# A gate for the first MLP's blocks: waiting for converted weights instead of converting in front of them

## The chip, the cores and the metric

The kernel runs on one core of a Trainium2 chip. The metric is the device time of one execution in microseconds (us). Engine names are those of the profile: PE (TensorE, matmuls), PEld (its weight loads), DVE (VectorE), ACT (ScalarE), POOL (GpSimd), SP (SyncE, which issues most DMAs). Each engine works through its own queue in order.

## What is computed

A linear recurrence over 768 steps for 4 x 8 heads of size 40, then two MLPs over 3072 tokens of width 320 with 2048 hidden units. In the reference's words, cut:

```python
for t in range(S):
    y[t] = r[t] @ state
    state = state * w[t] - outer(state @ a[t], b[t]) + outer(v[t], k[t])
x = y as (3072, 320)
x = (max(x @ w_in1, 0) ** 2) @ w_out1
h = x @ w_in2
return (h * clip(h + 3, 0, 6) / 6) @ w_out2
```

The weights come in as float64 and are converted to pairs of float32 on the chip: a high part and a low part.

## The kernel before, in words

**The recurrence** is cut into 12 chunks of 64 steps for each of 4 batches, 48 steps of a loop over `i`. One turn of that loop is called a *slot* here. A slot holds stages in the order of a string, `ORDER`: `rhs`, `ys` (of the slot before), `umm`, `f1`, `kt`, `pre`, `gmm`, `mp`, `st`, `vumm`, `mx`; `f1`, `kt` and `pre` prepare a slot that comes eight later. Between them stand four places `M`. The PE instructions of `rhs` (L670) are the first of a slot. ACT copies their result (RHS, L672) for `umm` (L680); ACT and DVE make GV (L700, L691) for `ys` (L710). Every four slots a triangular inverse is computed on DVE (L627, L630; ML, INV, TMP), in 62 small steps that are dealt out over the places.

**The first MLP** is cut into 6 groups of 512 tokens (each is the output of 8 slots) and 16 blocks of 128 hidden units. For a block there are two pieces: the first product (`project_in`, 8 matmuls into h, then r, g and gs on ACT and DVE), called IN here, and the second (`out1`, 8 matmuls into three accumulators o), called OUT. `piece()` issues one of the two; `fill(i)` calls it at each place `M`. `load` fetches a group's tokens (xr), `prep` splits them (`split_x`: xm, xh on ACT, L207 and L209). Before any group is ready, or while it is held, `fill` issues idle products instead (`keep_warm`, 4 at each place); once a group is ready an empty place stays empty.

**The conversion** (`convert`) is a generator over 32 items: 16 blocks, w_in and w_out of each (part 0 and 1). An item is a raw load (bits, on SP), five to seven elementwise steps on DVE, ACT and POOL (L127 to L156), and a store of the low part (LI or LO, in DRAM). It yields about four times an item, and two steps of it are taken at each place `M`. The first 16 items (blocks 0 to 7) run in slots 0 to 7, with scratch of their own. From block 8 on an item waits until the MLP has come near its block, since its low part goes straight into the tile (wd) that the matmuls will read, and that has two buffers. Later groups load the low parts again from DRAM (wl, L169, on ACT's queue), two blocks ahead.

`ahead` gets the weights of the block two further on, and through `block_in` and `block_out` calls `need`: if that block isn't converted, `need` takes as many steps of the generator as it lacks, on the spot. So around blocks 8 to 15 two to four items are issued in one go, in the middle of a slot.

After the recurrence the pieces follow each other alone, first the rest of the first MLP, then the second MLP (the same with its own weights); the second conversion starts when 94 INs of the first MLP are out.

Of the kernel before, what the change touches and what calls it, by code (L numbers as in the profile page):

```python
# [25 lines left out]
NF = 16  # L26
# [7 lines left out]
class Moe:  # L34


    def __init__(self, tc, ctx, pctx, consts):
        nc = self.nc = tc.nc
        self.pool = ctx.enter_context(tc.tile_pool(name="m_buf", bufs=1))
        self.rot = ctx.enter_context(tc.tile_pool(name="m_rot", bufs=2))  # L40
        self.pso = pctx.enter_context(tc.tile_pool(name="m_pso", bufs=1, space=PSUM))
        self.psh = pctx.enter_context(tc.tile_pool(name="m_psh", bufs=1, space=PSUM))
        self.xpool = ctx.enter_context(tc.tile_pool(name="m_x", bufs=2))
        self.hold = 0
        self.pso4, self.gpool, self.depth = None, self.rot, 2
        self.plan, self.wi, self.wo, self.gs = [], {}, {}, {}
        self.loaded, self.early, self.age = deque(), 0, 0
        self.aside, self.steps = iter(()), 0
        self.pairs = {}
        self.ready = self.n_in = self.n_out = self.s_in = self.s_out = 0  # L50
        self.cst = self.pool.tile([128, 36], FP32, name="cst")
        nc.sync.dma_start(out=self.cst, in_=consts["cst"])
# [233 lines left out]
    def ahead(self, n_in, n_out):  # L286
# [5 lines left out]
        while self.s_out <= min(n_out, len(self.plan) - 1):  # L292
            g, raw, f = self.plan[self.s_out]
            self.wo[self.s_out] = self.block_out(raw, f)
            self.s_out += 1

    def piece(self):

        n, o = self.n_in, self.n_out
        if self.loaded:  # L300
            self.loaded[0]["age"] -= 1
        if self.hold and self.ready:
            self.hold -= 1
        self.try_prep()
        if self.hold and self.ready:
            return False
        first = self.early == 0 and n % NF == 0 and o < n
        if n < self.ready and n - o < self.depth and not first:
            g, _, f = self.plan[n]
            self.gs[n] = self.project_in(self.wi.pop(n), g["x"], g["second"], lambda: self.ahead(n + 2, -1))  # L310
            self.n_in += 1
            self.try_prep()
        elif o < n:
            g, _, f = self.plan[o]
            if f == 0:
                g["acc"] = [self.acc(k, g["second"]) for k in range(4 if g["second"] else 3)]
            (self.out2 if g["second"] else self.out1)(g["acc"], self.wo.pop(o), self.gs.pop(o), f)
            if f == NF - 1:
                g["finish"](g["acc"])
            self.n_out += 1  # L320
            self.ahead(-1, o + 2)
        else:
            return False
        for _ in range(self.steps):
            next(self.aside, None)
        return True
# [126 lines left out]
def rwkv_moe_moe2_kernel(ctx, tc, pre_in, vr_in, v_in, nat, ident_d, mask_d, cst_d, w1_in, w1_out, w2_in, w2_out, out,  # L453
# [4 lines left out]
    NCH, NB = pre_in.shape[0], pre_in.shape[1]  # L458
# [7 lines left out]
    moe = Moe(tc, ctx, mctx, consts)  # L466
# [62 lines left out]
    def load_main(i):  # L529
        c, b = divmod(i, NB)  # L530
        for h, P in enumerate((PA, PB) if i < NS else ()):
            PV = slice(64, 128) if h == 0 else slice(0, 64)
            nc.sync.dma_start(out=VS[i % NB][PV, :, h, :], in_=v_in[c, b, h])
            nc.sync.dma_start(out=VR[i % 3][P, :, :, 64 - 64 * h:128 - 64 * h], in_=vr_in[c, b, h])
# [223 lines left out]
    def tick(n=1):  # L758
        for _ in range(n):
            if not gens or gens[0][1]:  # L760
                return
            if skip[0]:
                skip[0] -= 1
                return
            step = next(gens[0][0], "end")
            if step == "end":
                gens.popleft()
                done[0] += 1
                start_inv()
            elif step:  # L770
                gens[0][1] = step

    def slot_end():
        if gens and gens[0][1] > 0:
            gens[0][1] -= 1
# [14 lines left out]
    def pre_a():  # L790
        if jj[0] < NS:
            f1(jj[0])

    def pre_b():
        if jj[0] < NS:
            kt(jj[0])

    def pre_c():
        j = jj[0]
        if j >= NS:  # L800
            return
        adv(j + 1)
        if j % NB == NB - 1:
            gens.append([inv_gen(j // NB), None])
            start_inv()
        jj[0] += 1
# [7 lines left out]
    def fill(i):  # L814
        if not moe.piece() and (moe.ready == 0 or moe.hold):
            keep_warm(idle if i else 0)

    def store1(g):
        def go(acc):
            for k in range(3):  # L820
                o = moe.rot.tile([128, TOK], FP32, tag="rgr"[k], name="os")
                (nc.vector.tensor_copy if k % 2 else nc.scalar.copy)(out=o, in_=acc[k])  # L822
                nc.sync.dma_start(out=X2[g][128 * k:128 * k + 128], in_=o)
        return go
# [13 lines left out]
    with tc.manual_schedule():  # L838
# [33 lines left out]
        def cstep(n):  # L872
            for _ in range(n):
                next(moe.aside, None)
# [57 lines left out]
        groups1 = [moe.group(raw1, X1[g], 0, store1(g)) for g in range(NG)]  # L932
        STAGES = {"rhs": rhs, "umm": umm, "gmm": gmm, "vumm": vumm, "ys": ys, "st": st, "mp": merge_p, "mx": merge_x}

        def need_inv(i):
            while done[0] <= i // NB:
                if gens[0][1]:
                    slot_end()
                tick()

        for i in range(NS + 1):
            for word in (ORDER if moe.ready else ORDER0).split():
                name, _, off = word.partition(":")
                k = i + int(off or 0)
                if name == "M":
                    fill(i)
                    slot_end()
                    for k in range(5):
                        tick()
                        if k < 2:  # L950
                            cstep(1)
                elif name == "load":
                    if 0 <= k <= NS:
                        load_main(k)
                elif name == "f1":
                    pre_a()
                elif name == "kt":
                    pre_b()
                elif name == "pre":
                    pre_c()  # L960
                elif 0 <= k < NS:
                    if name == "mp":
                        need_inv(k)
                    STAGES[name](k)
                    if name == "ys" and k % (2 * NB) == 2 * NB - 1:
                        moe.load(groups1[k // (2 * NB)])
                        if k < 2 * NB:
                            moe.loaded[0]["age"] = 6
            if i == 2 * NB - 1:
                moe.need(raw1, n_early)  # L970
        actx.close()
        wp2 = ctx.enter_context(tc.tile_pool(name="m_w2", bufs=1))
        hctx = ctx.enter_context(ExitStack())
# [83 lines left out]
def build(arrays):  # L1057
    import concourse.bacc as _bacc
    import concourse.tile as _tile
    from concourse import mybir as _mybir  # L1060

    nc = _bacc.Bacc("TRN2", target_bir_lowering=False, num_devices=1)
    args, ins = [], {}
    for name in _INS:
        a = arrays[name]
        ins[f"in_{name}_dram"] = a
        args.append(nc.dram_tensor(f"in_{name}_dram", a.shape, _mybir.dt.from_np(a.dtype), kind="ExternalInput").ap())
    args.append(nc.dram_tensor("out_0_dram", (3072, 320), _mybir.dt.float32, kind="ExternalOutput").ap())
    with _tile.TileContext(nc) as tc:
        rwkv_moe_moe2_kernel(tc, *args[:3], args[3:9], *args[9:])  # L1070
    return nc, ins
# [8 lines left out]
```

## Time and profile before

| | |
|---|---|
| median of 3 runs | 1436.09 us (1433.65 to 1438.65) |
| the profiled execution | 1440.75 us |
| its span | 1439.0 us |
| PE busy | 1186.5 us, 82% |
| DVE, ACT, POOL busy | 55%, 42%, 28% |
| mean granted clock of PE | 0.895 |

A row of the page gives shares over the whole span; the stages have different bounds. A granted clock of 1.0 is 2.4 GHz, 0.5 is 1.2 GHz. PE's busy time counts pipelined matmuls whose ends are modelled.

### The profile page before, as it was taken

What the parts mean: (1) busy time and instruction counts of PE and PEld (TensorE: products, weight loads), DVE (VectorE), ACT (ScalarE), POOL (GpSimd) and SP (SyncE); (2) the same over time, 40 slices, a digit from 0 to 9 for tenths busy, and PEclk for the clock granted to TensorE, in tenths of its full rate; (3) what the DMA queues carried; (4) which work ended last, traced back from release to release, by engine and by line L of the source; (5) the groups of instructions that cost most, each with busy time, mean ns of one, the idle gap of its engine ahead of it and who ended that gap; (6) DMA issues with size and microseconds to landing.
All of it is one profiled execution on the core that took longest, in us unless ns stands there. A gap on an engine that the chain in (4) does not pass through costs nothing.

```text
span 1439.0 us, 25925 instructions
## 1 busy us (share of the span) xinstructions
PE 1186.5 (82%) x9682; PEld 1003.3 (70%) x9682; DVE 792.5 (55%) x1841; ACT 610.6 (42%) x1456; POOL 409.4 (28%) x612
## 2 busy tenths in 40 slices
PE   3177787976679899999999899797666899999994
PEld 3166776855568677777778778585544798888984
DVE  7823667586575949575765733345554444344432
ACT  4144443535445445445444433344444433344331
POOL 5685454344534333333332000003333000000000
PEclk9668689987689999999999999898778999999997
DMA  5534556636537475665655442634333443434331
GB/s 127 135 79 132 124 123 141 145 94 145 131 95 164 104 143 150 138 122 137 140 133 107 128 111 76 213 110 149 121 112 99 135 130 118 138 104 136 102 118 50
DMA packets 270150, 178.43 MB, mean 124 GB/s; under 512 B 202944, under 2 KB 228160, under 8 KB 270016
## 3 DMA queue, kind: packets, MB, share of 16 engines
q1 hardware_dynamic: 238656, 106.95, 32.5%
q10 hardware_dynamic: 29312, 63.45, 14.7%
q0 software_dynamic: 2048, 6.29, 1.1%
q8 instruction: 79, 1.29, 0.4%
q14 instruction: 55, 0.45, 0.1%
HBM read 140.99 MB, written 35.65 MB: 123 GB/s over the span
## 4 chain that ended last, share of the span: by engine, by line
PE 36%; DVE 13%; DMA 11%; ACT 4%; POOL 3%; issue 3%; SPq 1%; ACTq 0%; DVEq 0%; POOLq 0%
PE h L221 7%; PE h L223 3%; PE o L261 3%; DMA DT<-TB 3%; DMA wl<-LO 3%; PE o L262 3%; DMA wl<-LI 3%; PE o L260 2%; DVE TMP L627 2%; DVE INV L630 2%; PE o L248 2%; POOL cv L139 2%; PE h L225 2%; PE h L224 2%; PE o L250 2%
## 5 line engine op out<-in xcount | busy, mean ns | idle before, releaser
L221 PE MATMUL h<-xm,wi_hi 128*128 128x512 f32 x384 | 165.9, 432 | 38.5 <-ACT wi_hi L70 38.5
L239 DVE TENSOR_TENSOR gs<-g,gs 128x512 fp32r<-128x512 f32 x192 | 143.8, 749 | 80.7 <-ACT gs L233 68.8
L221 PE MATMUL h<-xm,wl 128*128 128x512 f32 x336 | 134.5, 400 | 22.5 <-DMA wl<-LI 22.5
L627 DVE TENSOR_TENSOR TMP<-ML,INV 128x126 f32<-128x126 f32 (+22 forms) x341 | 109.7, 322 | 70.1 <-DMA ML<-DT 50.9
L596 POOL TENSOR_TENSOR RK<-RK,mask 64x256 f32<-64x256 f32 x96 | 74.0, 771 | 255.6 <-ACT RK L595 244.4
L231 DVE SCALAR_TENSOR_TENSOR g<-r,h 128x512 f32<-128x512 f32 x96 | 65.9, 686 | 124.5 <-ACT r L230 124.4
L236 DVE TENSOR_TENSOR g<-r 128x512 f32<-128x512 f32 x96 | 66.6, 694 | 112.1 <-ACT r L235 112.1
L260 PE MATMUL o<-wo_hi,gs 128*128 128x320 f32 x384 | 123.0, 320 | 4.8 <-ACT os L822 3.0
L262 PE MATMUL o<-wo_hi,gs 128*128 128x320 f32 x384 | 122.6, 319 | 1.9 <-DVE gs L239 1.9
L223 PE MATMUL h<-xr,wi_hi 128*128 128x512 f32 x384 | 123.2, 403 | 0.0
L230 ACT ACTIVATE r<-h,cst 128x512 f32<-128x512 f32 x96 | 66.0, 687 | 122.2 <-PE h L225 117.8
L139 POOL TENSOR_TENSOR cv<-bits,cv 128x384 int32<-128x384 int32 (+1 forms) x48 | 44.7, 931 | 254.2 <-DVE bits L127 183.4
L221 PEld LDWEIGHTS h<-xm,wi_hi 128*128 128x128 f32 x384 | 76.9, 200 | 49.9 <-ACT wi_hi L70 40.5
L630 DVE TENSOR_TENSOR INV<-INV,TMP 128x126 f32<-128x126 f32 (+22 forms) x341 | 106.7, 313 | 7.9
L235 ACT ACTIVATE r<-h 128x512 f32<-128x512 f32 x96 | 57.2, 596 | 104.7 <-PE h L225 95.1
L261 PE MATMUL o<-wl,gs 128*128 128x320 f32 x320 | 99.9, 312 | 0.4
L233 ACT CAST gs<-g 128x512 fp32r<-128x512 f32 x96 | 59.5, 620 | 71.7 <-DVE g L231 71.7
L221 PEld LDWEIGHTS h<-xm,wl 128*128 128x128 f32 x336 | 64.1, 191 | 34.9 <-DMA wl<-LI 26.6
L223 PEld LDWEIGHTS h<-xr,wi_hi 128*128 128x128 f32 x384 | 75.1, 196 | 17.6
L248 PE MATMUL o<-gs,wo_hi 128*128 128x512 f32 x192 | 86.9, 452 | 0.0
L557 POOL TENSOR_TENSOR RK<-IN,EE 40x256 f32<-40x256 f32 x82 | 69.8, 852 | 57.6 <-DVE EE L545 54.3
L260 PEld LDWEIGHTS o<-wo_hi,gs 128*128 128x128 f32 x384 | 74.9, 195 | 14.1 <-ACT gs L233 6.6
(174 smaller groups left out, 2763.8 us busy)
## 6 DMA issues: line engine op xcount, KB each, us to landing
wl<-LI ACTq DMA_DIRECT2D x84, 384.0 KB
IN<-in_pre_dram SPq DMA_DIRECT2D x44, 418.0 KB
wl<-LO ACTq DMA_DIRECT2D x44, 384.0 KB
wl<-LO ACTq DMA_DIRECT2D x40, 320.0 KB
bits<-in_moe_w_in_dram SPq DMA_DIRECT2D x32, 384.0 KB
bits<-in_moe_w_out_dram SPq DMA_DIRECT2D x32, 320.0 KB
VR<-in_vr_dram SPq DMA_DIRECT2D x96, 80.0 KB
DT<-TB SPq DMA_DIRECT2D x24, 256.0 KB
```

The costliest lines, as they stand in the source:

```text
L139: nc.gpsimd.tensor_tensor(out=q, in0=t.bitcast(I32), in1=q, op=ALU.add)
L221: nc.tensor.matmul(h, w[p][:, k], xm[:, k], start=(k + p == 0), stop=False)
L223: nc.tensor.matmul(h, hi[:, k], lo[:, k], start=False, stop=False)
L239: nc.vector.tensor_tensor(out=gs[:, 1], in0=g, in1=gs[:, 0].bitcast(FP32), op=ALU.subtract)
L248: nc.tensor.matmul(acc[d], hi, gs[:, 0], start=a, stop=False)
L260: nc.tensor.matmul(acc[q], gs[:, 0, s], hi, start=a, stop=False)
L261: nc.tensor.matmul(acc[q], gs[:, 0, s], lo[:, 0:DM], start=False, stop=False)
L262: nc.tensor.matmul(acc[q], gs[:, 1, s], hi, start=False, stop=z)
L557: e.tensor_tensor(out=rk[P, :, 64 * h:64 * h + 64], in0=a[P], in1=E[P, :, 0:64], op=ALU.mult)
L596: nc.gpsimd.tensor_tensor(out=o, in0=o, in1=mask[P].unsqueeze(1).to_broadcast([64, NP, 64]), op=ALU.mult)
L627: eng.tensor_tensor(out=tmp, in0=ml[:, s, s + 1:32].unsqueeze(2).to_broadcast([128, n, w]), in1=inv[:, s, 0:w].unsqueeze(1).to_broadcast([ ...
L630: eng.tensor_tensor(out=inv[:, s + 1:32, 0:w], in0=inv[:, s + 1:32, 0:w], in1=tmp, op=ALU.subtract)
```

## The change

A function `short(n, o)` says whether the weights of block n (first product) or o (second product) are not yet converted. `piece()` asks it for the two blocks that `ahead` would fetch and, as long as `gate` is set, issues nothing at that place if it says so; the conversion then goes on with its two steps a place. `gate` is cleared at the end of the recurrence. A group's tokens, which were loaded as soon as they were written, now wait in a list until all items are converted and the MLP has begun the group two before it.

```diff
+    def short(self, n, o):
+        for k, extra in ((n, 2), (o, 4)):
+            _, raw, f = self.plan[min(k, len(self.plan) - 1)]
+            if raw is self.raw and self.converted < 2 * (f - f % 2) + extra:
+                return True
+        return False
...
-        if self.hold and self.ready:
+        if self.hold and self.ready or self.gate and self.short(n + 2, o + 2):
             return False
...
                     if name == "ys" and k % (2 * NB) == 2 * NB - 1:
-                        moe.load(groups1[k // (2 * NB)])
-                        if k < 2 * NB:
-                            moe.loaded[0]["age"] = 6
+                        waiting.append(k // (2 * NB))
+
+                if waiting and (moe.converted == 2 * NF and moe.n_in >= (waiting[0] - 1) * NF or waiting[0] == 0):
+                    g = waiting.popleft()
+                    moe.load(groups1[g])
+                    if g == 0:
+                        moe.loaded[0]["age"] = 6
...
+        moe.gate = False
         actx.close()
```

**Place one: ACT between slots 13 and 14.** In the program before, from the end of a piece's conversion to the copy RHS of slot 14 (r and gs belong to an IN, bits, wi_hi and wd to the conversion, GV, TB and RHS to the recurrence):

```order
L138 ACTIVATE bits<-bits 128x384
L700 COPY GV_138<-a 128x8x40
L235 ACTIVATE r<-h 128x512
L237 ACTIVATE gs<-r 128x512
L130 ACTIVATE bits<-bits 128x384
L70 CAST wi_hi<-bits 128x384
L138 ACTIVATE bits<-bits 128x384
L70 CAST wi_hi<-bits 128x384
L663 ACTIVATE TB_129<-a 128x4x32
L672 COPY RHS_137<-a 128x160
```

The same place in the changed program, up to the next copies of the recurrence (its lines are 8 further on):

```order
L235 ACTIVATE r<-h 128x512
L237 ACTIVATE gs<-r 128x512
L708 COPY GV_138<-a 128x8x40
L130 ACTIVATE bits<-bits 128x320
L671 ACTIVATE TB_129<-a 128x4x32
L680 COPY RHS_137<-a 128x160
L138 ACTIVATE bits<-bits 128x320
L690 ACTIVATE VR_136<-a 40x4x64 x2
```

Of the four conversion steps between GV and RHS one is left; the others stand in later slots.

**Place two: ACT where the recurrence ends.** Before: the last copy GV, and the split of group 5 (xm, xh) two INs later.

```order
L700 COPY GV_138<-a 128x8x40
L235 ACTIVATE r<-h 128x512
L237 ACTIVATE gs<-r 128x512
L169 DMA wl<-LI_7_206 128x768
L235 ACTIVATE r<-h 128x512
L237 ACTIVATE gs<-r 128x512
L169 DMA wl<-LO_7_214 128x768
L207 CAST xm<-xr 128x512 x2
L209 CAST xh<-xr 128x512
L235 ACTIVATE r<-h 128x512
L237 ACTIVATE gs<-r 128x512
L169 DMA wl<-LI_0_199 128x768
```

In the changed program the last copy GV is followed by blocks of group 4:

```order
L708 COPY GV_138<-a 128x8x40
L235 ACTIVATE r<-h 128x512
L237 ACTIVATE gs<-r 128x512
L169 DMA wl<-LI_1_200 128x768
L830 COPY os<-o_8140 128x512
L830 COPY os<-o_8142 128x512
L235 ACTIVATE r<-h 128x512
L237 ACTIVATE gs<-r 128x512
L169 DMA wl<-LO_1_208 128x768
```

and the split of group 5 stands in the middle of that group's blocks:

```order
L169 DMA wl<-LI_4_203 128x768
L169 DMA wl<-LO_3_210 128x768
L235 ACTIVATE r<-h 128x512
L237 ACTIVATE gs<-r 128x512
L207 CAST xm<-xr 128x512 x2
L209 CAST xh<-xr 128x512
L235 ACTIVATE r<-h 128x512
L237 ACTIVATE gs<-r 128x512
L169 DMA wl<-LI_5_204 128x768
```

Twelve INs and twelve OUTs more stand behind the recurrence than before; the loads of weights and the split go with them.

## Rows read from the trace of the kernel before

**Rows 1.** The page's 40 slices: PE busy and PE's granted clock, in tenths.
```profile
PE   3177787976679899999999899797666899999994
PEclk9668689987689999999999999898778999999997
```
**Rows 2.** Timeline of PE: start, us, instruction; first of slots 0, 8, 12, 23.
```profile
71.93 0.97 PE L670 MATMUL a<-VS,RK 128*64 128x40 f32 x14
...
216.53 0.66 PE L670 MATMUL a<-VS,RK 128*64 128x40 f32 x16
...
280.36 0.67 PE L670 MATMUL a<-VS,RK 128*64 128x40 f32 x16
...
508.93 0.66 PE L670 MATMUL a<-VS,RK 128*64 128x40 f32 x16
```
**Rows 3.** Stretches between slots: length, busy times, PE's clock, DMA share, GB/s.
```profile
core 0: us, PE busy (x) PEld busy (x) DVE busy (x) ACT busy (x) POOL busy (x), PEclk, DMA share, GB/s
71.90:216.50 144.60, 113.66 (x1182) 102.34 (x1180) 69.06 (x183) 62.34 (x184) 86.54 (x132) 0.73 0.48 114
136.40:216.50 80.10, 61.18 (x625) 55.16 (x624) 49.81 (x138) 32.71 (x97) 42.39 (x60) 0.74 0.51 116
216.50:247.40 30.90, 24.43 (x315) 22.00 (x314) 21.89 (x66) 13.42 (x42) 12.25 (x22) 0.94 0.63 137
280.40:508.90 228.50, 179.55 (x1718) 148.50 (x1716) 156.69 (x400) 109.92 (x293) 96.59 (x132) 0.85 0.54 125
299.50:429.80 130.30, 89.72 (x784) 74.30 (x781) 90.52 (x225) 63.34 (x165) 59.94 (x77) 0.76 0.49 118
429.80:492.00 62.20, 59.17 (x628) 49.05 (x624) 42.29 (x112) 31.92 (x87) 24.01 (x37) 0.97 0.61 142
```
**Rows 4.** PE's waits in 299.5 to 429.8: total us, times, longest.
```profile
PE a L680 <- ACT RHS L672: 28.0, 5, 6.1
PE a L710 <- ACT GV L700: 11.3, 4, 3.1
```
**Rows 5.** Timeline of ACT in slot 13; in brackets idle before and releaser.
```profile
304.54 0.55 ACT L70 CAST wi_hi<-bits 128x384 fp32r<-128x384 f32 x1 [0.72 <-DVE bits L146]
...
308.72 0.54 ACT L70 CAST wi_hi<-bits 128x384 fp32r<-128x384 f32 x1 [3.16 <-DVE bits L146]
...
309.34 0.28 ACT L672 COPY RHS<-a 128x160 f32<-128x160 f32 x1
```
**Rows 6.** Groups of DVE in 280 to 430, by line and shape: busy us, mean ns.
```profile
L239 DVE TENSOR_TENSOR gs<-g,gs 128x512 fp32r<-128x512 f32 x12 | 10.0, 836 | 0.9
L236 DVE TENSOR_TENSOR g<-r 128x512 f32<-128x512 f32 x12 | 8.7, 723 | 3.7 <-ACT r L235 3.7
```
**Rows 7.** DVE's waits in 429.8 to 558.9.
```profile
DVE TMP L627 <- DMA ML<-DT: 17.2, 2, 8.8
```
**Rows 8.** DVE's waits in 136.4 to 216.5.
```profile
DVE bits L127 <- issue: 9.3, 1, 9.3
...
DVE bits L156 <- DMA LO<-bits: 7.0, 1, 7.0
DVE bits L127 <- DMA LI<-bits: 5.8, 1, 5.8
```
**Rows 9.** Timeline of PE after the recurrence: the first matmuls of two INs.
```profile
933.62 0.39 PE L221 MATMUL h<-xm,wi_hi 128*128 128x512 f32 x1
...
937.25 0.39 PE L221 MATMUL h<-xm,wi_hi 128*128 128x512 f32 x1
```
**Rows 10.** PE's waits in 898 to 925.
```profile
PE h L221 <- DMA wl<-LI: 10.2, 1, 10.2
```
**Rows 11.** Timeline of ACT in 903 to 924.
```profile
905.80 1.14 ACT L207 CAST xm<-xr 128x512 fp32r<-128x512 f32 x2 [4.45 <-DMA xr<-X]
908.45 0.62 ACT L209 CAST xh<-xr 128x512 fp32r<-128x512 f32 x1 [1.51 <-DMA xr<-X]
...
909.60 0.34 ACTq L169 DMA_DIRECT2D wl<-LI  x1
```

More of the change, by code (lines that the diff above doesn't have):

```diff
@@ L43, in __init__ @@
         self.xpool = ctx.enter_context(tc.tile_pool(name="m_x", bufs=2))
-        self.hold = 0
+        self.hold, self.gate = 0, True
         self.pso4, self.gpool, self.depth = None, self.rot, 2
@@ L933, in rwkv_moe_moe2_kernel @@
         STAGES = {"rhs": rhs, "umm": umm, "gmm": gmm, "vumm": vumm, "ys": ys, "st": st, "mp": merge_p, "mx": merge_x}
+        waiting = deque()
         def need_inv(i):
```

## The prediction

> **What bounds the kernel now.** I read the page's slices first: PE is busy eight or nine tenths in most slices from the thirteenth on, but six and seven tenths in slices nine to twelve, where its granted clock is lower too [rows 1]. To tell what lies there I took the starts of the first PE instruction of a slot, the rhs products (L670), as marks [rows 2], and asked for the stretches between such marks [rows 3]. A slot is one turn of the loop over `i`; it has four places for a piece of the first MLP, a first product (8 matmuls, called IN below) or a second product (OUT). Four slots without conversion (429.8 to 492.0) take 62.2 us at a clock of 0.97: PE is the bound there. The five slots from 299.5 take 130.3 us at 0.76, with PE busy 89.7. Who ended PE's waits there stands in [rows 4]: ACT, 39.3 us, at the copies RHS (L672) and GV (L700). The reason stands in ACT's own rows [rows 5]: it waits 3.16 us at L70 for the DVE's half of a conversion step, and the RHS copy that PE needs is queued behind that. So in this stretch the conversion of blocks 8 to 15, forced in bulk between two pieces, stands in front of the recurrence, and PE, whose queue is in order, does nothing else meanwhile. After the recurrence PE runs the MLPs back to back: what is taken out of the slots must be done there.
>
> **The change part by part.** The gate is decided while the program is written; it adds no instruction and no semaphore wait. The first difference in the order is in slot 12, and in slots 12 to 22 (280.4 to 508.9) the new program has 10 INs and 10 OUTs where the old one has 22 of each; the 16 items of conversion (eight blocks, two parts) are all in these slots in both. From slot 23 on every slot has its four pieces again, and the missing 12 INs and 12 OUTs stand after the last attention instruction. Each engine has as many instructions as before. So there are three terms.
>
> *First term, slots 12 to 22, now 228.5 us [rows 3].* Not shown by the trace is a slot with scattered conversion, about one pair of pieces and no idle products, so I bound it. From below: DVE is busy 156.7 us here; the 12 INs that leave take a g (0.723) and a gs (0.836) each [rows 6], 18.7 us, and 138.0 stay. Three inverses begin in the stretch, and DVE waits 17.2/2 = 8.6 us for ML at each [rows 7]: 163.8 us if it never idles otherwise. From above: slots 4 to 7, with two items each and no MLP, take 80.1/4 = 20.0 us [rows 3]; eleven of them are 220. The nearest rows are slots 0 to 9. Slots 8 and 9 convert nothing: 30.9/2 = 15.45 us. Slots 0 to 7 convert 16 items: 144.6 less 8 x 15.45 = 123.6 leaves 21.0 us for them. Eleven slots and 16 items at these prices are 170.0 + 21.0 = 191.0. Two corrections: the early items write their low parts through scratch that waits for its stores, 7.0 and 5.8 us of DVE, and 9.3 more without a named releaser [rows 8]; later items write theirs into the tile that the matmuls read. I take off 12.8 and half of 9.3, 17.5 in all. And the ten INs bring DVE 10 x 1.56 = 15.6 us, of which I count the share in which DVE was busy in slots 0 to 7, 69.1/144.6 = 0.48: 7.5. That gives 181.0 us, 16.5 a slot, and a gain of 47.5; the ends are 64.7 and 8.5.
>
> What is queued behind what: in the new order at most a few conversion instructions stand between two copies of ACT that PE waits for, so the waits of [rows 4] become shorter and more numerous, and DVE, which carries inverse, conversion and gs, is late next. POOL is busy 96.6 of 228.5 us and keeps its work; the DMA engines are busy 0.54 [rows 3], so the later loads of raw weights hide.
>
> *Second term, after the attention.* Two INs there start 937.25 - 933.62 = 3.63 us apart [rows 9], with an OUT between them and PE never idle, at the full clock. Twelve pairs more: +43.6 us. Nothing covers this; PE is the chain there. Its low-part loads are issued two blocks ahead as now. The second MLP's conversion waits until block 94 in both programs, so it gets no earlier cover from these pairs and costs what it costs.
>
> *Third term, the stall at the hand-over.* PE now stands still 10.2 us for wl<-LI [rows 10]. That load was issued at 909.60, behind the split of group 5 (L207, L209), which waited 4.45 and 1.51 us for xr [rows 11], the last output of the attention on its way back. With 12 more blocks of group 4 to do, that split comes five blocks after the attention's end, when xr has landed. I take the 5.96 us that the issue was late; the ends are 0 and the whole 10.2, since the raw weights of the second MLP are still loaded at the same time.
>
> Moved without a price: the loads and splits of groups 1 to 4 fall into other slots. Group 1's load goes from slot 16 to 22, past SP's loads of six slots, and needs a buffer that the conversion leaves. A split that waits for xr again costs up to the 5.96 us of [rows 11], one that stops waiting gains as much; I take nothing and keep both ends. The stores of X2 come later; the second MLP reads them long after.
>
> Sum: -47.5 + 43.6 - 6.0 = -9.9. The profiled execution took 1440.75 us (span 1439.0): 1430.9. It lies 4.66 us above the median of the runs, 1436.09, so I forecast 1426 us for the median. A difference under 0.3%, 4.3 us, can't be told from none. Each us by which the stretch differs from 181 moves the time by one.
>
> **The rivals.** *The clock takes it back (slower).* Four pieces a slot are also what keeps PE at 2.4 GHz. With half of them gone, and no idle products issued in the empty places since a group is ready, PE waits oftener, and what follows a wait runs at 1.2 GHz. The place is slots 12 to 22; the price is that of slots 4 to 7, at a clock of 0.74, 20.0 us a slot: 220 us, a gain of 8.5, and -8.5 + 43.6 - 6.0 = +29, 1465 us. It decides from a stretch of 195 us on, 17.7 a slot. For it: slots 0 to 7 ran at 0.73 although idle products filled their places. Against it: slots 8 and 9, also without MLP, ran at 0.94, so the low clock goes with the waits of the early conversion, a part of which won't recur. The Trainium skill, "TensorE: Matmul & The Clock Gate", section "HAM oscillation — how this bites in real kernels", speaks for this rival: bursts of matmuls with waits between them start cold again and again, and its advice is to keep work in one piece. The trace agrees so far that the five slots with the long waits have 0.76 and the four without them 0.97 [rows 3]; whether shorter waits cost less no row here shows.
>
> *An even exchange.* The 24 pieces cost 43.6 at the end, and the slots give back about as much: a stretch of 187 to 195 us, 1432 to 1440. For it: 191.0 without my corrections. Against it: the scratch waits are named in the trace and their cause is gone.
>
> *DVE alone decides (faster still).* If scattered steps hide entirely, the stretch goes to 163.8, the stall goes as a whole: -64.7 + 43.6 - 10.2 = -31.3, 1405 us. Against it: DVE was busy no more than 70% of any stretch in [rows 3] that holds conversion.
>
> That blocks are still forced in front of the products is excluded by the order: the long runs of conversion on ACT are gone from these slots.
>
> **How the numbers follow.** Forecast, a stretch of 170 to 187, 1415 to 1432 us: 0.43. DVE alone, below 1415: 0.12. Even exchange: 0.22. The clock, above 1440: 0.23. So faster 0.55, same 0.22, slower 0.23. The range is 1406 to 1450: it leaves out a little of the DVE case and the outer half of the clock's. The forecast's own range is 1415 to 1432.
>
> **What would show it.** The first: the rhs products of slots 12 and 23 stand 181 us apart; PE's waits at L672's and L700's successors are no longer 5 us each; the mean clock of the stretch is above 0.8. A clock near 0.74 and slots of 20 us show the rival. The second: the attention's end 40 to 50 us earlier, and 12 more INs 3.6 us apart before the second MLP. The third: no 10 us wait of PE just after the attention, and the split of group 5 without a wait for xr. I am wrong if the attention's end moves by less than 33 us, or if the added pairs take much more than 3.63 us each.

## The result, and the profile after

The changed kernel takes 1447.14 us (median of 4 runs, 1445.71 to 1449.11); the kernel before, on the same chip, 1437.15 (1433.65 to 1438.65). The ratio is 1.0074 with a 95% interval of 1.0051 to 1.0097. The forecast was 1426 us, faster by 0.7%; the kernel is slower by 0.7%, though its time lies inside the stated range of 1406 to 1450. The profiled execution took 1445.71 us (span 1443.8, mean clock of PE 0.885), 4.96 us more than that of before.

By stages, cut at the first rhs products of slots 0, 8, 12, 23 and 40, the last matmul of the attention, the first IN of the second MLP and the end of the span (us):

| | 0 to 7 | 8 to 11 | 12 to 22 | 23 to 39 | 40 to 47 | to second MLP | second MLP |
|---|---|---|---|---|---|---|---|
| before | 144.6 | 63.8 | 228.6 | 277.0 | 112.1 | 79.1 | 461.8 |
| after | 141.3 | 64.5 | 197.6 | 277.1 | 111.1 | 116.2 | 463.5 |

So everything happened where the prediction looked: slots 12 to 22, called *the stretch* below, are 31.0 us shorter, and what follows the attention is 37.1 longer. The part up to the second MLP, before and after, by windows with columns as in [rows 3]:

```profile
898.00:977.10 79.10, 68.92 (x298) 56.62 (x297) 31.53 (x49) 28.74 (x49) 3.48 (x4) 0.94 0.50 158
```
```profile
864.10:980.30 116.20, 112.50 (x490) 92.67 (x489) 48.18 (x73) 43.52 (x73) 3.50 (x4) 0.99 0.46 155
```

The page's slices of after (PE busy and granted clock, tenths) answer [rows 1]; the stretch is slices nine to fourteen:

```profile
PE   4177878968577898999899998997667899999995
PEclk9667788978687999999999999998767999999998
```

PE is less busy in the stretch than before and at a lower clock. The same stages by windows, columns as in [rows 3], are slots 0 to 7, the stretch, and slots 23 to 39:

```profile
72.60:213.90 141.30, 111.19 (x1184) 99.90 (x1182) 67.66 (x178) 62.18 (x183) 83.01 (x130) 0.74 0.48 115
278.30:475.90 197.60, 143.42 (x1529) 121.18 (x1525) 138.83 (x374) 93.33 (x267) 92.47 (x131) 0.77 0.50 116
475.90:753.00 277.10, 253.63 (x2658) 209.95 (x2654) 186.76 (x480) 135.03 (x366) 101.72 (x155) 0.96 0.57 133
```

DVE has 138.83 us of work left, within a microsecond of the 138.0 that the prediction worked out; PE has lost 36.1 us of work but the stretch only 31.0. PE's waits in the stretch (total us, times, longest), which answer [rows 4], are:

```profile
PE a L718 <- ACT GV L708: 31.1, 7, 7.3
PE a L688 <- ACT RHS L680: 7.3, 4, 2.7
PE a L744 <- DVE TMP L635: 6.5, 2, 3.6
```

They add up, with smaller ones, to 54.1 us, against 48.9 in before's stretch. The long wait for RHS has gone; in its place stands GV (L708; L700 before). How such a wait looks is seen in the timeline at 386 (start, us, instruction; in brackets idle before and releaser):

```profile
386.71 0.55 DVE L135 SCALAR_TENSOR_TENSOR cv_t<-bits,cv_t 128x384 uint32<-128x384 uint32 x1
387.29 0.55 ACT L138 ACTIVATE bits<-bits 128x384 f32<-128x384 f32 x1 [6.57 <-DVE cv_t L135]
387.75 0.40 ACT L708 COPY GV<-a 128x320 f32<-128x320 f32 x1
...
388.20 1.13 PE L718 MATMUL a<-GV,KT 128*64 128x104 f32 x10 [7.34 <-ACT GV L708]
```

ACT's Abs of a conversion item (L138) waits 6.57 us for the DVE's step before it, the copy GV is queued behind it, and PE waits 7.34 us. That is the pattern of [rows 5] again, with one item instead of several. DVE had not been idle meanwhile. In the 12.7 us up to the end of that step and the small one behind it, it was busy for 12.38 (third of the busy times):

```profile
374.70:387.40 12.70, 5.83 (x73) 4.93 (x72) 12.38 (x34) 5.98 (x19) 6.11 (x9) 0.77 0.29 85
```

Steps of the inverse (TMP, INV), g and gs and the slot's own stages stood in DVE's queue ahead of the step that ACT waited for. What DVE itself waits for in the stretch stands in its groups (busy us, mean ns, idle before and releasers):

```profile
L635 DVE TENSOR_TENSOR TMP<-ML,INV 128x126 f32<-128x126 f32 (+22 forms) x93 | 28.6, 308 | 13.0 <-DMA ML<-DT 11.4
L146 DVE SCALAR_TENSOR_TENSOR bits<-bits 128x384 f32<-128x384 f32 (+1 forms) x16 | 8.8, 548 | 12.5 <-POOL bits L139 12.5
L127 DVE TENSOR_SCALAR cv_t<-bits 128x384 uint32<-128x384 uint32 (+1 forms) x16 | 5.9, 367 | 20.1 <-DMA bits<-in_moe_w_out_dram 12.1 <-DMA bits<-in_moe_w_in_dram 8.0
```

The same group in the kernel before, in its stretch from 280.4 to 508.9:

```profile
L127 DVE TENSOR_SCALAR cv_t<-bits 128x384 uint32<-128x384 uint32 (+1 forms) x16 | 7.2, 448 | 4.9 <-DMA bits<-in_moe_w_in_dram 4.9
```

So DVE now stands 20.1 us for raw weights that are still under way, where it stood 4.9. After the attention (PE's wait; starts of the first matmuls of two INs), for [rows 10] and [rows 9]:

```profile
PE h L221 <- DMA wl<-LI: 3.7, 1, 3.7
```
```profile
886.02 0.39 PE L221 MATMUL h<-xm,wi_hi 128*128 128x512 f32 x1
...
889.65 0.39 PE L221 MATMUL h<-xm,wi_hi 128*128 128x512 f32 x1
```

The stall is 3.7 us instead of 10.2, and a pair of pieces costs 3.63 us as before.

### The profile page after: what moved, and what is told of

The parts are those of the page before. It is cut to its first block, busy times and chain, and to the rows that moved or that the text cites. A ratio compares the mean times of both kernels' runs of the same rounds, so it can differ in the third digit from the quotient of the medians.

```text
span 1443.8 us, 25927 instructions
## 1 busy us (share of the span) xinstructions
PE 1197.8 (83%) x9682; PEld 1016.8 (70%) x9682; DVE 794.9 (55%) x1841; ACT 609.0 (42%) x1456; POOL 407.9 (28%) x612
## 4 chain that ended last, share of the span: by engine, by line
PE 36%; DVE 13%; DMA 11%; ACT 3%; POOL 3%; issue 2%; SPq 1%; DVEq 0%; ACTq 0%; POOLq 0%
PE h L221 8%; PE h L223 4%; DMA wl<-LI 4%; DMA DT<-TB 3%; PE o L261 3%; PE o L262 3%; PE o L260 3%; DVE INV L638 2%; DVE TMP L635 2%; PE h L225 2%; PE h L224 2%; PE o L248 2%; POOL cv L139 2%; PE o L250 2%; PE o L249 2%
## 5 line engine op out<-in xcount | busy, mean ns | idle before, releaser
L221 PE MATMUL h<-xm,wi_hi 128*128 128x512 f32 x384 | 165.5, 431 | 34.2 <-ACT wi_hi L70 34.2
L635 DVE TENSOR_TENSOR TMP<-ML,INV 128x126 f32<-128x126 f32 (+22 forms) x341 | 106.2, 311 | 66.6 <-DMA ML<-DT 59.6
L260 PE MATMUL o<-wo_hi,gs 128*128 128x320 f32 x384 | 124.6, 324 | 4.8 <-ACT os L830 3.0
L139 POOL TENSOR_TENSOR cv<-bits,cv 128x384 int32<-128x384 int32 (+1 forms) x48 | 44.8, 933 | 289.5 <-DVE bits L127 218.7
L262 PE MATMUL o<-wo_hi,gs 128*128 128x320 f32 x384 | 124.1, 323 | 1.4 <-DVE gs L239 1.4
L235 ACT ACTIVATE r<-h 128x512 f32<-128x512 f32 x96 | 57.3, 597 | 141.3 <-PE h L225 108.5
L221 PEld LDWEIGHTS h<-xm,wi_hi 128*128 128x128 f32 x384 | 77.3, 201 | 46.2 <-ACT wi_hi L70 36.2
L718 PE MATMUL a<-GV,KT 128*64 128x104 f32 (+1 forms) x768 | 53.6, 291 | 58.1 <-ACT GV L708 37.1
L718 PEld LDWEIGHTS a<-GV,KT 128*64 128x64 f32 (+1 forms) x768 | 42.5, 147 | 71.8 <-ACT GV L708 38.6
```

The costliest lines, as they stand in the source:

```text
L139: nc.gpsimd.tensor_tensor(out=q, in0=t.bitcast(I32), in1=q, op=ALU.add)
L221: nc.tensor.matmul(h, w[p][:, k], xm[:, k], start=(k + p == 0), stop=False)
L260: nc.tensor.matmul(acc[q], gs[:, 0, s], hi, start=a, stop=False)
L262: nc.tensor.matmul(acc[q], gs[:, 1, s], hi, start=False, stop=z)
L635: eng.tensor_tensor(out=tmp, in0=ml[:, s, s + 1:32].unsqueeze(2).to_broadcast([128, n, w]), in1=inv[:, s, 0:w].unsqueeze(1).to_broadcast([ ...
L718: nc.tensor.matmul(ps[P, p, :], ktt[:, p, P], gv[:, p, h, :], start=(p == 0), stop=False)
```

## The experiments

The theories for the stretch: **clock** (PE runs at 1.2 GHz in a thinned stage), **ACT order** (Abs in front of GV), **DVE work**, **raw loads** (a load is asked for too late), and, for what these leave, the **steps of the conversion** as a whole. Ratios are to the kernel before on the same chip, with 95% intervals. Line numbers below are those of the changed kernel.

| | ratio | stretch, us | its clock |
|---|---|---|---|
| changed kernel, again | 1.0054 [1.0031, 1.0077] | 201.6 | 0.75 |
| clock: idle products | 1.0077 [1.0051, 1.0104] | 201.2 | 0.86 |
| ACT: Abs late | 1.0044 [1.0027, 1.0061] | 201.3 | 0.76 |
| ACT: Abs and split late | 1.0053 [1.0031, 1.0074] | 200.1 | 0.79 |
| DVE: merge left out | 1.0037 [1.0012, 1.0061] | 200.7 | 0.75 |
| loads: POOL's queue | 1.0064 [1.0039, 1.0088] | 199.5 | 0.76 |
| loads: fourth buffer | 0.9964 [0.9946, 0.9983] | 190.7 | 0.77 |
| the same again | 0.9996 [0.9974, 1.0017] | 191.3 | 0.78 |
| fourth buffer, five steps left out | 0.9905 [0.9880, 0.9930] | 174.6 | 0.81 |
| no gate, fourth buffer | 0.9960 [0.9933, 0.9986] | 226.3 | 0.86 |
| the same again | 0.9956 [0.9936, 0.9977] | 225.5 | 0.84 |

### The changed kernel again

> The changed kernel once more, unaltered, as a measure for the runs beside it: 1.003 to 1.010 of the kernel before, by every theory.

1.0054, a stretch of 201.6 and a tail (from the attention's end to the second MLP) of 115.9: the result stands, and stretches of three-buffer versions are to be compared with 197.6 to 201.6.

### The clock

In the empty places that the gate makes, the idle products are issued:

```diff
-        if not moe.piece() and (moe.ready == 0 or moe.hold):
+        if not moe.piece() and (moe.ready == 0 or moe.hold or moe.gate):
```

> The changed kernel with four idle products on PE (as in slots 0 to 9) at every place that the gate leaves empty. Clock theory: the mean clock of slots 12 to 22 rises from 0.77 to 0.88 or more and the stretch falls from 197.6 to 175 to 187 us, the time to 1426 to 1438. Queue theory: PE's waits for GV stay (25 to 35 us) and the stretch stays within 5 us of 197.6 or grows by the products' own time. DVE theory: as the queue theory.

1.0077. The stretch (columns as in [rows 3]):

```profile
279.10:480.40 201.30, 158.74 (x1722) 138.45 (x1719) 139.24 (x374) 93.19 (x267) 91.96 (x130) 0.86 0.51 114
```

The clock is back at the level of before (0.86, and 0.85 before), and the stretch hasn't become shorter. But the idle products have a price of their own on PE (busy us, mean ns, idle before and releaser):

```profile
L820 PE MATMUL h<-ident 128*128 128x128 f32 x192 | 31.0, 312 | 7.1 <-ACT r L235 7.1
```

They take 31.0 us of PE's time. The kernel's own products, added up by tile (a, h, o), took 139.7 us instead of 150.0, and PE's idle time fell from 54.2 to 42.6 us. So the run shows that idle products bring nothing here; what a higher clock would bring without them it doesn't show. The clock rival's own price, 20.0 us a slot, did not come: the stretch took 18.0.

### ACT's order

Abs of a late item (blocks 8 to 15) is issued beside the next item's first step; in a second version the high copy of the split comes a step after L146 too (cut; the step kept in `later` is issued behind L130 of the next item):

```diff
-                nc.scalar.activation(out=m, in_=high.bitcast(FP32), func=ACTF.Abs)
+                later.append(lambda m=m, high=high: nc.scalar.activation(out=m, in_=high.bitcast(FP32), func=ACTF.Abs))
```

> The changed kernel, with the Abs of a late conversion item (ACT, L138) issued two steps later, beside the next item's first ACT step, so that ACT no longer waits there for DVE's L135. Nothing else moves; the gate closes at the same places. In the changed kernel PE waits 31.1 us for the copy GV in slots 12 to 22, and ACT 35.5 us at L138 for DVE. Queue theory (one conversion step that waits for DVE's backlog stands ahead of GV on ACT, and PE waits with it): GV waits fall from 31.1 to under 12 us, the stretch of slots 12 to 22 from 197.6 to 175 to 185 us, the time from 1447 to 1426 to 1436. DVE theory (DVE is the bound and any wait is only renamed): PE waits for STK, TMP or GV of DVE instead, the stretch stays within 5 us. Clock theory (PE at 1.2 GHz is what costs): waits fall, but the mean clock stays under 0.8 and the stretch gains under 8 us.

> As the run before, and the copy of a late item's high part (ACT, L70 or L74) with what follows it also comes one step after DVE's L146 instead of right behind it. Queue theory: ACT's waits at L70 and L74 (35.1 us in the changed kernel) fall by more than half, and the stretch of slots 12 to 22 gains another 3 to 10 us. DVE theory: no further gain, within 3 us. Clock theory: no further gain.

1.0044 and 1.0053. PE's waits of the first version (its lines are shifted by up to four):

```profile
PE a L722 <- DVE GV L703: 19.5, 5, 5.4
PE a L692 <- ACT RHS L684: 14.5, 5, 4.5
PE a L748 <- DVE STK L734: 8.6, 4, 3.3
```

The 31.1 us for ACT's GV have shrunk to 5.9, but the DVE's half of GV, ACT's copy RHS and DVE's STK have taken over and the sum is 57.1 instead of 54.1. Of the wait for GV, ACT only passed on that DVE was late. The same edit on the kernel before did nothing:

> The kernel before, with the same later Abs and no gate. Queue theory: ACT's wait at L138 (25.6 us in 299 to 430) goes, but steps forced in bulk still wait for each other (L70 and L74 for L146, L146 for POOL), so PE's waits of 39.3 us fall by a quarter to a half and the time gains 4 to 15 us, 1422 to 1433. DVE theory: no change, within 4 us. Clock theory: no change beyond the waits that go, under 8 us.

1.0008 [0.9986, 1.0029].

### DVE's work

The merge at L135 is left out for late items, so their low bits are not the reference's:

```diff
-            nc.vector.scalar_tensor_tensor(out=t, in0=high, scalar=0xC0000000, in1=t, ...)
+            if own:
+                nc.vector.scalar_tensor_tensor(out=t, in0=high, scalar=0xC0000000, in1=t, ...)
```

> The changed kernel without L135, the second DVE step of the 16 late conversion items (its effect on the weights of blocks 8 to 15 is left out); 9.7 us of DVE less (0.61 us each), nothing else moves. The later Abs renamed PE's waits from ACT to DVE and left their sum (54 to 57 us) and the stretch as they were. DVE theory (in slots 12 to 22 DVE's queue is always either busy, 138.8 us, or waiting, 55.8, and PE follows it): the stretch falls by 8 to 12 us from 197.6, and PE's waits by as much. Queue theory, as far as it is left: the stretch falls by under 4. Clock theory: under 4.

1.0037, and the stretch stays:

```profile
278.40:479.10 200.70, 145.87 (x1529) 123.88 (x1526) 136.37 (x359) 93.56 (x267) 93.70 (x132) 0.75 0.51 114
```
```profile
L127 DVE TENSOR_SCALAR cv_t<-bits 128x384 uint32<-128x384 uint32 (+1 forms) x16 | 6.5, 404 | 23.3 <-DMA bits<-in_moe_w_out_dram 12.3 <-DMA bits<-in_moe_w_in_dram 11.0
```

DVE gets to the raw weights earlier and waits for them longer, 23.3 us.

### The raw loads

`fill` asks for a load at the head of an item, and counts as finished only the item before the last: with three buffers the load of an item is asked for one item ahead, with four two. In the trace of the changed kernel the loads go out in pairs, one right behind the other: DVE uses the first of a pair 3.4 to 5.8 us after its issue, the second after 16 to 29 us. All its six waits for raw weights are at a first one. With the fourth buffer no load issued in the stretch is used sooner than 12 us after its issue.

```diff
-                return 4 if k < n_early else 3
+                return 4 if k < n_early or k > n_early + 2 else 3
...
-                late_scratch.append([cp.tile([128, 768], U32, name="bits"), x[:, 0], x[:, 1]])
+                late_scratch.append([cp.tile([128, 768], U32, name="bits"), x[:, 0], x[:, 1], cp.tile([128, 768], U32, name="bits_d")])
...
-            return late_scratch[what][k % (3 - what)]
+            return late_scratch[what][k % (2 if what else 4)]
```

> The changed kernel with a fourth buffer for the raw weights of late items, so that a raw load is issued one item earlier. DVE waits 20.1 us for raw weights (L127) in slots 12 to 22 of the changed kernel. DVE theory: that wait falls under 6 us, the stretch by 8 to 16 us, the time to 1431 to 1439. Queue theory: PE's waits and stretch stay within 4 us, since ACT's waits for DVE remain. Clock theory: no change.

0.9964. The stretch, and DVE's reads of raw weights (two groups, since the fourth buffer has its own name):

```profile
282.80:473.50 190.70, 142.82 (x1528) 121.65 (x1524) 140.41 (x374) 92.94 (x267) 93.49 (x132) 0.77 0.52 119
```
```profile
L127 DVE TENSOR_SCALAR cv_t<-bits 128x384 uint32<-128x384 uint32 (+1 forms) x12 | 5.1, 421 | 0.0
...
L127 DVE TENSOR_SCALAR cv_t<-bits_d 128x320 uint32<-128x320 uint32 x4 | 1.3, 320 | 0.0
```

The waits are gone as a whole, and the stretch is 6 to 11 us shorter at the same clock (190.7 and 191.3 against 197.6 and 201.6), with ACT's order and DVE's work as they were. What shrank is PE's idle time, 197.6 - 143.4 = 54.2 to 190.7 - 142.8 = 47.9 us, and not its work. Of the theories tried up to here it is the only one that moves the stretch. That another queue doesn't do it was shown by sending the late raw loads through POOL's:

```diff
-            nc.sync.dma_start(out=bits, in_=(w_out if part else w_in)[f])
+            (nc.gpsimd if w["second"] == 0 and f >= direct else nc.sync).dma_start(out=bits, in_=(w_out if part else w_in)[f])
```

> The changed kernel with three raw buffers as it has, but the raw loads of late items issued on POOL's queue instead of SP's. In the changed kernel these loads stand on SP behind loads IN<-in_pre, which wait for DVE and POOL (49.6 us of SP's waits in slots 12 to 22), and DVE then waits 20.1 us for raw weights. Queue-of-SP theory: DVE's waits for raw weights fall under 8 us, the stretch by 4 to 12 us, the time to 0.995 to 1.002 of the kernel before, as with a fourth buffer. Landing theory (with three buffers a load simply starts too late, whatever its queue): the waits stay over 14 us and the time over 1.003.

1.0064; DVE still waits 14.1 us:

```profile
L127 DVE TENSOR_SCALAR cv_t<-bits 128x384 uint32<-128x384 uint32 (+1 forms) x16 | 6.2, 388 | 14.1 <-DMA bits<-in_moe_w_out_dram 10.0 <-DMA bits<-in_moe_w_in_dram 4.0
```

So SP's queue holds back a part (20.1 to 14.1), and the stretch, 199.5 us, gains nothing by it. The rest is lead: on POOL's queue, which is in order too, the late loads took 5 to 8 us to land.

### What is left with four buffers

Once the loads are in place, each of the other suspects was lifted again, with the edits from above.

> The changed kernel with the fourth raw buffer, and without the step at L135 (the DVE's merge of the rounding bits) for the late items, so that the low halves of these weights are not the reference's. With four buffers the gated stretch took 190.7 us and DVE no longer waited for raw weights; these 16 merges took 7.2 + 2.0 = 9.2 us of it. If DVE's own work is what is late once the loads are there, the stretch falls to 181 to 184 and the ratio to about 0.991; if something else in the chain is late (POOL's half of the conversion, the transposed copies ML that DVE waits 15.9 us for), DVE waits that much longer, the stretch stays at 188 to 192 and the ratio at 0.996.

> The changed kernel with the fourth raw buffer, and idle products also in the places that the gate leaves empty. With three buffers these raised the clock from 0.77 to 0.86 and the time did not fall, but PE then waited for DVE, which waited for loads. If the clock is late once the loads are there, the stretch falls from 190.7 to 180 to 185 at a clock above 0.85 and the ratio to 0.990 to 0.993; if not, the stretch stays at 189 to 194 and the ratio is 0.996 to 0.999.

> The changed kernel with the fourth raw buffer, and ACT's Abs of a late item issued beside the next item's first step, so that the copies that PE needs no longer stand behind it. With four buffers PE still waited 32.6 us for the copy GV behind that Abs. If ACT's order is late once the loads are there, the stretch falls from 190.7 to 175 to 185 and the ratio to 0.987 to 0.993; if ACT only hands on DVE's lateness, as with three buffers, the waits change their names, the stretch stays at 188 to 194 and the ratio at 0.996 to 0.998.

0.9984 [0.9966, 1.0003], 1.0013 [0.9990, 1.0035] and 1.0015 [0.9992, 1.0037]. The stretches, in this order:

```profile
280.40:469.90 189.50, 143.19 (x1526) 121.72 (x1524) 136.64 (x359) 92.85 (x267) 94.12 (x132) 0.77 0.53 119
```
```profile
281.60:474.50 192.90, 158.01 (x1722) 137.90 (x1718) 140.78 (x374) 93.24 (x267) 93.98 (x132) 0.87 0.52 117
```
```profile
283.60:476.30 192.70, 142.54 (x1528) 121.62 (x1526) 139.60 (x375) 93.60 (x267) 93.82 (x132) 0.77 0.50 117
```

All lie within 2 us of 191, and the last two ratios lie above what was written down for an unchanged stretch. So neither the merge, 9 us of DVE's time, nor ACT's order holds the rest alone. For the clock the run says as little as before: its idle products take 30.7 us of PE's time. Then the steps together: for late items L127, L135, L138, L139 and L146 are left out (`if own:` in front of them), load, scaling and split stay, so these weights are not the reference's.

> The changed kernel with the fourth raw buffer, and without five of the steps of a late item (L127, L135, L138, L139, L146: the bit operations, Abs, POOL's sum and the last product); the load, the scaling at L130 and the split into high and low stay, so that these weights are not the reference's. Lifting one suspect at a time (DVE's merge, ACT's order, the clock) left the gated stretch at 189 to 193 us. If the steps of an item together, each handing to the next engine between the recurrence's own steps, are what the stretch pays beside the recurrence, most of the 21 us of my count 11 x 15.45 + 21 = 191 go: a stretch of 170 to 178 and a ratio of 0.985 to 0.990. If the recurrence with its ten pairs of products alone sets the stretch, it stays at 186 to 191 and the ratio at 0.995 to 0.998.

0.9905, a stretch of 174.6, at a clock of 0.81 instead of 0.77 (here the window ends on the mark of slot 23):

```profile
280.70:455.40 174.70, 130.70 (x1530) 112.34 (x1526) 120.98 (x326) 86.02 (x251) 75.72 (x116) 0.81 0.55 129
```

Without the five steps the stretch is 16 us shorter, 1.0 us an item. DVE lost 19.4 us of work by it (140.41 to 120.98), ACT 6.9 and POOL 17.8, and which of these the stretch pays for is not shown: DVE idled 50 us in it, and the merge alone, 9 us, changed nothing. Nor is the clock's part separated: 12.1 of the 16 us are a shorter busy time of PE for the same products (142.82 to 130.70), 3.9 its waits. These are still 44.0 us, most of them for DVE (line numbers one further on):

```profile
PE a L719 <- DVE GV L700: 19.8, 6, 6.2
PE a L745 <- DVE TMP L636: 17.4, 3, 8.6
```

### The fourth buffer without the gate

> The kernel before, without a gate, with the fourth raw buffer. DVE waits 4.9 us there for raw weights in 280 to 430, so by both theories it gains 0 to 5 us: 0.996 to 1.001 of the kernel before. If it gains 8 us or more, the fourth buffer and not the gate is what made the gated kernel with four buffers faster than before.

> The changed kernel with the fourth raw buffer, unaltered from bits4, beside old4_again on the same chip. If the gate is worth nothing once the loads are there, the two come out within 0.2% of each other, both at 0.995 to 0.998; if the gate is still a loss, this one is slower by 0.3% or more; if it is a gain, faster by as much.

> The kernel before the change with the fourth raw buffer, unaltered from old_bits4, on the same chip as bits4_again: 0.995 to 0.998 if the fourth buffer helps without the gate as it did before, and within 0.2% of bits4_again if the gate is an even exchange; lower than that by 0.3% or more if the gate costs time even with the loads in place.

The kernel before with the fourth buffer takes 0.9960 and 0.9956 of its time; it beats both kernels, 1434.31 and 1435.01 us. The gated one came out at 0.9964 on one chip and at 0.9996 on another, beside the ungated one. On one chip the gate therefore costs about 0.4% even with the loads in place (the intervals share only 0.9974 to 0.9977), which was one of the outcomes written down; by the first pair, 0.9964 and 0.9960 on two chips, it was even. The stages say why there is no gain: 225.5 - 191.3 = 34.2 us less in the stretch, 117.9 - 77.3 = 40.6 more after the attention.

### Two other ways out of the price

`short` asked only for the block of the piece that is due, so that fewer places stay empty:

```diff
-        if self.hold and self.ready or self.gate and self.short(n + 2, o + 2):
+        if self.hold and self.ready:
             return False
...
+        go_in = n < self.ready and n - o < self.depth and not first
+        if self.gate and (self.short(n + 2, 2) if go_in else o < n and self.short(o + 2, 4)):
+            return False
```

> The changed kernel with the gate asked only for what the next piece itself will fetch (first product: w_in two blocks on; second: w_out), so fewer places stay empty: at the end of slot 22 two INs and three OUTs more are done (17 and 16 instead of 15 and 13). DVE theory: the stretch grows by their DVE work and no more, 3 to 6 us, the tail loses five pieces of 1.82 us, 9.1 us: 3 to 6 us faster than the changed kernel. Clock theory: the stretch gets shorter too, 8 us or more faster in all. Queue theory: as the DVE theory.

1.0049 [1.0026, 1.0073], not the 3 to 6 us less than the changed kernel that were written down. The stretch took 201.5 us. The tail fell to 107.2 as it should, but slots 23 to 47 took 13 us more (283.9 + 117.7 against 277.1 + 111.1), with as many pieces in them as in the changed kernel. Why was not settled. And 20 instead of 16 early items, without and with the gate (and four buffers; cut, the call that forces the early items also moves from slot 7 to slot 8):

```diff
-                         lag=8, n_early=16, depth=3, idle=4):
+                         lag=8, n_early=20, depth=3, idle=4):
```

> The kernel before, no gate, but the first 20 items (blocks 0 to 9) converted early through DRAM, the last four of them in slot 8, before the MLP starts; 12 items stay forced instead of 16. If a forced item costs PE 2.8 to 3.5 us where it stands (all theories): slots 13 to 17 lose 4 items, 11 to 14 us; slot 8 grows by what four items cost there, DVE theory 4 x 1.9 to 4 x 2.8 (8 to 11 us), clock theory 0 to 4. So DVE theory 0 to 5 us faster than before, clock theory 8 to 14 us faster.

> The gated kernel with four raw buffers, and the first 20 items instead of 16 converted early, as in the ungated run: nine pairs of pieces are moved behind the recurrence instead of twelve (10.9 us less there), the early items cost about 10 us in slot 8 (slots 8 to 11 took 74.4 us instead of 63.8 in the ungated run), and twelve late items instead of 16 leave slots 12 to 22 with more pieces. All theories: about even with four buffers alone, 0.993 to 1.000 of the kernel before.

1.0007 [0.9983, 1.0030] and 1.0021 [1.0003, 1.0039]. In the first, slots 8 to 11 take 74.4 us instead of 63.8 and the stretch 218.2 instead of 228.6: 10.6 lost, 10.4 won. Four items forced in slot 8 cost what four forced later cost, 2.6 us each. The second lies above the 0.993 to 1.000 that were written down for it.

## Why the prediction was wrong

**First term, wrong in size: -47.5 forecast, -31.0 measured.** The stretch took 197.6 us instead of 181.0, and these 16.6 us are more than the whole gain forecast, 9.9. Two steps failed.

*"so the later loads of raw weights hide"*, argued from a DMA share of 0.54. A share says that the engines have room; it doesn't say that a load is asked for in time. With the items spread over the places DVE waits 20.1 us for loads that were issued 3.4 to 5.4 us before their use. The fourth buffer, which takes just this wait away, shortens the stretch by 6 to 11 us; with slots 8 to 11, whose length varies from one profile to the next, by 4 to 7. By the ratios (0.9964 and 0.9996 against 1.0074 and 1.0054) it gives 8 to 16 us, and the loss against the kernel before is gone. This step the runs show.

*The two corrections, -17.5 and +7.5.* With the loads in place the stretch is 190.7 and 191.3; the sum before the corrections was 191.0 (11 slots at 15.45 and 21.0 for 16 items). I had taken 17.5 us off for scratch waits of the early items, as if the path were shortened by every wait of DVE that goes. That the early scratch waits lay beside the path is what these numbers suggest; it was not tried by itself, and the plain sum may have met the measurement by luck, since its 15.45 us a slot were read at a clock of 0.94 and the stretch ran at 0.77.

*"so the waits of [rows 4] become shorter and more numerous"*: half wrong. One item is enough for a long wait. PE's waits for ACT's copies RHS and GV went from 39.3 us in 9 waits, the longest 6.1, to 38.4 in 11, the longest 7.3, and all its waits together from 48.9 to 54.1 in a shorter stretch.

**Second and third terms, right.** 12 pairs at 3.63 us and a smaller stall give 43.6 - 6.5 = 37.1, and the tail grew by 116.2 - 79.1 = 37.1. The stall fell from 10.2 to 3.7 where I took 5.96 off, and the split of group 5 no longer waits for xr, as forecast. The sign by which the prediction would have called itself wrong did not catch the miss: the attention's end came 33.9 us earlier (898.0 to 864.1), just above the bound of 33, and 33.9 does not pay for 37.1.

**The rivals.** The sum of the profile is -31.0 + 37.1 = +6.1, of which 4.8 stand in the spans; the forecast for the profile was -9.9. The medians are 21 us from the forecast, 6 more than the profiles, because the profiled execution lay 4.66 us above the median before and 1.43 below it after; that is scatter of the executions. The even exchange (187 to 195) is what the kernel with the fourth buffer shows; the kernel as changed lay at 197.6, above the 195 from which I had the clock rival decide. So the time lies in the part of the range that was kept for that rival, and that it lies in the range is no credit to the forecast. The low clock of the rival was there (0.77), but the loss went with the fourth buffer at the same clock (0.77 and 0.78), so the raw loads account for it without the clock. Whether a higher clock would have saved as much is not shown. The Trainium skill, "TensorE: Matmul & The Clock Gate", section "HAM oscillation — how this bites in real kernels", treats a cold clock after waits as a cost to be avoided by unbroken work. Here the clock went from 0.75 to 0.86 in the run with idle products and the stretch from 201.6 to 201.2, with 31.0 us of idle products in it; no run here shows what unbroken work would give.

**Open.** What the clock alone costs in the stretch: no run raised it without giving PE more work or taking steps out. Whether the order on DVE decides: in the wait shown at 386 the step stood behind steps of the inverse, and without the five steps PE still waits 19.8 us for DVE's GV; no run moved the inverse. Which part of the five steps the stretch pays for although DVE idles 50 us beside them (it waits for ML 15.9, POOL's sum 14.5 and r 7.0 in the run with four buffers). Why the fourth buffer gives the ungated kernel 0.4% where DVE waited only 4.9 us for raw weights in the stretch (the stretch gives 2.3 and 3.1 us). And the 13 us in slots 23 to 47 of the split question.

## What to carry to other kernels

Work taken out of a stage with waits and put behind it, where PE never waits, is paid there in full (3.63 us a pair here): the move pays only if the stage shrinks by more than that, so price the stage from its own undisturbed slots and leave a plain sum uncorrected unless a run supports the correction. When a bulk step is scattered, look at how far ahead its loads are asked for, not at the share of the DMA engines. A wait named after one in-order engine may only hand on another's: move the named instruction, and see whether the sum of waits falls or only the names change.

## What the runs showed of the hardware

In the changed kernel's stretch DVE waited for six raw loads of 320 or 384 KB, and began to read them 3.4 to 5.4 us after their issue. Two of these, the issue on SP and then the step of DVE that waited:

```profile
384.66 0.35 SPq L94 DMA_DIRECT2D bits<-in_moe_w_in_dram  x1
...
408.82 0.49 SPq L94 DMA_DIRECT2D bits<-in_moe_w_out_dram  x1
```
```profile
390.00 0.36 DVE L127 TENSOR_SCALAR cv_t<-bits 128x384 uint32<-128x384 uint32 x1 [2.58 <-DMA bits<-in_moe_w_in_dram]
```
```profile
413.68 0.33 DVE L127 TENSOR_SCALAR cv_t<-bits 128x320 uint32<-128x320 uint32 x1 [7.08 <-DMA bits<-in_moe_w_out_dram]
```

That is 5.3 and 4.9 us from issue to use. On POOL's queue the profile gives the landing itself (KB each, median us to landing):

```profile
bits<-in_moe_w_in_dram POOLq DMA_DIRECT2D x8, 384.0 KB, 6.3
bits<-in_moe_w_out_dram POOLq DMA_DIRECT2D x8, 320.0 KB, 5.8
```

The Trainium skill, "DMA: Bandwidth & Descriptors", section "Anatomy of one DMA — SWDGE (gpsimd) path", gives a fixed 2.0 us and the bytes at 436 GB/s, from which an estimate for 384 KB is 2.9 us; beside the other traffic of this stretch the measured 6.3 us are twice that, and the measurement decides.
